# Query projections of a fused attention and feed-forward kernel in bursts of eight heads

## The chip, the cores and the metric

The kernel runs on one core of a Trainium2 chip. The engines of that core have instruction streams of their own: TensorE (PE in the profile, with its weight loads listed as PEld), VectorE (DVE), ScalarE (ACT), GpSimd (POOL) and SyncE (SP, which here only issues DMAs). The metric is the time of one execution on the device, in microseconds (us); lower is better. Before the change it is 561.32 us, the median of three runs from 560.52 to 561.76.

## What is computed

```python
def reference(A_x, A_k_cache, A_v_cache, A_wq, A_wo, B_x, B_w_gate, B_w_up, B_w_down):
    ...
        W = min(4096, max(256, Sk // 4))            # 512
        rep = Hq // Hkv                             # 16 // 8
        q = (x @ wq).reshape(B, Sq, Hq, Dh)         # 2048 rows, 16 heads of 256
        k = jnp.repeat(k_cache[:, :, Sk - W:, :], rep, axis=1)
        v = jnp.repeat(v_cache[:, :, Sk - W:, :], rep, axis=1)
        scores = jnp.einsum("bhqd,bhkd->bhqk", q, k) * (Dh ** -0.5)
        p = softmax(scores, axis=-1)
        o = jnp.einsum("bhqk,bhkd->bhqd", p, v)
        return o.reshape(B, Sq, Hq * Dh) @ wo
    ...
    xn = _layernorm(x, axis=-1)                     # x is 2048 x 448
    s = _A_ref(xn, A_k_cache, A_v_cache, A_wq, A_wo)
    g = _silu((gelu(xn @ w_gate) * (xn @ w_up)) @ w_down)
    return x + s * g
```

Every row of x attends to the last 512 cached keys; two query heads share one key head. The attention result is multiplied by a gate from a feed-forward net and added to x.

## The kernel before

The 2048 rows are worked in four chunks of 512 (QC), each as four tiles of 128 rows (TPC). The first part of the program (about 127 us) is the layer norm and the feed-forward net: `gate_up` (matmuls L370) and `down` (L382) leave the gate's input in `gy`. `silu` (L499 on ACT, L500 and L502 on POOL) turns it into the gate, one tile at a time, during the attention part.

The attention part is one loop over i = 0 to 63: chunk c = i // 16, head i % 16. For each i, four steps t = 0 to 3 are written out by hand, in this order for TensorE:

- `scores(i, t)`: two matmuls (L420) of 128 query rows against 512 keys, into PSUM bank 4 or 5. ACT takes the exponentials and their row sum (L424) into one of NPR row buffers `pr`, DVE takes the reciprocal (L426) and scales the row buffer in place (L427), and SP issues a DMA transpose (L236) from the row buffer into `pT`. Each row buffer has its own DMA semaphore.
- at even t, from the third head on, `values` for a head two and a half heads back: four matmuls (L440) of the transposed probabilities with V, into a bank from a table of eight places (0, 6, 0, 6, 0, 1, 6, 6). DVE empties it into `oT` (L446).
- at odd t, from i = 6, half of `outproj`: four of the eight matmuls (L460) that multiply a group of four finished heads by wo, for one tile of rows, in bank 7. When the second half is through (t = 3), DVE copies or adds the bank to `acc` (L479, L481). After a chunk's last group POOL multiplies by the gate (L485) and adds the rows of x (L487) from the buffer `xr` into `ofin`. After the fourth tile POOL issues the store of the chunk's result and the load of the next chunk's rows into `xr` (`load_xr`, issued through L233).
- at t = 0 of every fourth head, i = 3, 7, ..., 59, `q_burst`: the queries of the next four heads. A burst has four units. A unit is 14 matmuls of 64 contracted rows (L406); they come in pairs that run side by side in the two halves of the array and fill two PSUM banks, 0 and 1 or 2 and 3. ACT copies both banks with one instruction of 1024 columns (L410) into `qT`, which holds six heads. One burst also stands before the loop.

The outputs of the last group of all (chunk 3, heads 12 to 15) are written out after the loop, with smaller DVE instructions (L469, L471) that write `ofin`, and stores of their own. Before them the loop's remaining five `values` and two `outproj` follow (L549 to L553).

Nothing is scheduled by a planner: each engine runs its instructions in the order of the source. `Rec` (L23) records every operation with the tiles it reads and writes, and puts semaphore waits where an operation needs another engine's result or a buffer that another engine still uses; a DMA that overwrites a tile waits for DMAs and engines that read it. Buffers of the attention part lie in the SBUF space of buffers of the feed-forward part.

Of the kernel before, what the change touches and what calls it, by code (L numbers as in the profile page):

```python
# [5 lines left out]
ACT = mybir.ActivationFunctionType  # L6
ALU = mybir.AluOpType
BF16 = mybir.dt.bfloat16
# [3 lines left out]
P = 128  # L12
# [129 lines left out]
def bass_recurrent_scan__sliding_block_cached__geglu_ffn__prompt_kernel(nc, A_x, A_k, A_v, A_wq, A_wo, B_x, B_wg, B_wu, B_wd, out):  # L142
    _, S, D = A_x.shape
    Hkv, Sk, Dh = A_k.shape[1], A_k.shape[2], A_k.shape[3]
    HD = A_wq.shape[1]
    Hq = HD // Dh
# [12 lines left out]
    with es:  # L159
        off = [16512]  # L160

        def sb(name, shape, dt, at=None):
            n = 4 if dt == F32 else 2
            for x in shape[1:]:
                n *= x
            if at is None:
                at = off[0]
                off[0] += (n + 31) // 32 * 32
            return R.place(name, shape, dt, at), at + (n + 31) // 32 * 32
# [24 lines left out]
        hb, ffn_end = sb("hb", [P, NHB, QC], BF16)  # L194


        NPT = 4
        qT, at = sb("qT", [P, 6, NE, QC], BF16, gu_at)
        oT = [None, None]
        oT[0], at = sb("oT0", [P, 4 * NE, QC], BF16, at)  # L200
        xr, at = sb("xr", [P, TPC, D], BF16, at)
        assert at <= x_at
        pT, at = sb("pT", [P, NPT, NJ, QC], BF16, x_at)
        pr = []
        while at + 2 * W <= d_at:
            t_, at = sb("pr%d" % len(pr), [P, W], BF16, at)
            pr.append(t_)
        at = hb_at
        while at + 2 * W <= ffn_end:
            t_, at = sb("pr%d" % len(pr), [P, W], BF16, at)  # L210
            pr.append(t_)
        NPR = len(pr)
        oT[1], at = sb("oT1", [P, 4 * NE, QC], BF16, d_at)
        acc, at = sb("acc", [P, TPC, D], F32, at)
        tmp, at = sb("tmp", [P, 2, D], F32, at)
        ofin, at = sb("ofin", [P, TPC, D], BF16, at)
        assert at <= hb_at, (at, hb_at)
        psum = es.enter_context(nc.psum_tensor("ps", [P, 8 * 512], F32))

        def bank(b, n=512):  # L220
            return psum[:, b * 512:b * 512 + n]
# [10 lines left out]
        def dma(eng, dst, src, w=(), r=(), after=(), lane=None):  # L232
            return R.op(eng, lambda e: e.dma_start(dst, src), r=r, w=w, dma=True, after=after, lane=lane)  # L233
# [159 lines left out]
        NI = NQC * Hq  # L393
        NG = NI // 4

        def q_burst(G):

            c, h0 = divmod(4 * G, Hq)
            for n in range(4):
                hp, e_ = divmod(n, 2)  # L400
                s, i = 2 * (n % 2) if G else (4, 0, 2, 0)[n], (4 * G + 2 * hp) % 6

                def run(e, hp=hp, e_=e_, s=s):
                    for k in range(NK):
                        for b, lo in ((s, 0), (s + 1, HP)):
                            ins = e.matmul(bank(b), lhsT=wq[lo:lo + HP, k, h0 // 2 + hp, e_ * P:(e_ + 1) * P],  # L406
                                           rhs=xnT[lo:lo + HP, c, k, :], start=k == 0, stop=k == NK - 1)
                    return ins
                pe(run, r=xn(c) + [("wq", lo, k) for lo in range(2) for k in range(NK)], w=[("ps", s), ("ps", s + 1)])
                act(lambda e, e_=e_, s=s, i=i: e.activation(  # L410
                    qT[:, i:i + 2, e_, :], psum[:, s * 512:(s + 2) * 512].rearrange("p (a q) -> p a q", a=2), ACT.Copy),
                    r=[("ps", s), ("ps", s + 1)], w=[("qT", i, e_), ("qT", i + 1, e_)])

        def scores(i, t):
            g, n = (i % Hq) // 2, i * TPC + t
            b, s = 4 + n % 2, n % NPR

            def run(e):
                for k in range(NE):
                    ins = e.matmul(bank(b), lhsT=qT[:, i % 6, k, t * P:(t + 1) * P], rhs=kT[:, g, k, :],  # L420
                                   start=k == 0, stop=k == NE - 1)
                return ins
            pe(run, r=[("kT", g), ("qT", i % 6, 0), ("qT", i % 6, 1)], w=[("ps", b)])
            act(lambda e: e.activation(pr[s][:, :], bank(b), ACT.Exp, scale=scale, accum_out=den[:, s:s + 1]),  # L424
                r=[("ps", b)], w=[("pr%d" % s,), ("den", s)])
            dve(lambda e: e.reciprocal(rden[:, s:s + 1], den[:, s:s + 1]), r=[("den", s)], w=[("rden", s)])  # L426
            dve(lambda e: e.tensor_scalar(pr[s][:, :], pr[s][:, :], rden[:, s:s + 1], None, op0=ALU.mult),  # L427
                r=[("pr%d" % s,), ("rden", s)], w=[("pr%d" % s,)])
            dmaT(pT[:, i % NPT, :, t * P:(t + 1) * P], pr[s][:, :], r=[("pr%d" % s,)], w=[("pT", i % NPT, t)], lane="p%d" % s)

# [19 lines left out]
        def outproj(G, t, part, half=None):  # L450

            n8 = 4 * NE
            lo, hi = (0, D) if half is None else (half * D // 2, (half + 1) * D // 2)
            b = ((2, 2), (3, 5), (7, 4), (0, 6))[t][half or 0] if G == NG - 1 else (7, 7, 7, 4)[t] if G == NG - 2 else 7
            c, h0 = divmod(4 * G, Hq)
            end = c == NQC - 1

            def run(e):
                for idx in part:
                    ins = e.matmul(bank(b, D)[:, lo:hi], lhsT=oT[G % 2][:, idx, t * P:(t + 1) * P],  # L460
                                   rhs=wo[:, h0 * NE + idx, lo:hi],
                                   start=idx == 0, stop=idx == n8 - 1)
                return ins
            pe(run, r=[("oT%d" % (G % 2), idx) for idx in part] + [("wo", h0 // 4)], w=[("ps", b)])
            if part[-1] < n8 - 1:
                return
            n = c * TPC + t
            if end and h0 == Hq - 4:
                dve(lambda e: e.tensor_tensor(tmp[:, t % 2, lo:hi], bank(b, D)[:, lo:hi], gy[:, n, lo:hi], ALU.mult),  # L469
                    r=[("ps", b), ("gy", n)], w=[("tmp", t % 2)])  # L470
                dve(lambda e: e.tensor_tensor(ofin[:, t, lo:hi], tmp[:, t % 2, lo:hi], acc[:, t, lo:hi], ALU.add),  # L471
                    r=[("tmp", t % 2), ("acc", t)], w=[("ofin", t, lo)])
                if t == TPC - 1:
                    dma("sync" if half else "scalar", o_view[:, c, t, lo:hi], ofin[:, t, lo:hi], r=[("ofin", t, lo)])
                elif half != 0:
                    dma("sync", o_view[:, c, t, :], ofin[:, t, :], r=[("ofin", t, 0), ("ofin", t, lo)])
                return
            if h0 == 0:
                dve(lambda e: e.tensor_copy(acc[:, t, :], bank(b, D)), r=[("ps", b)], w=[("acc", t)])  # L479
            else:  # L480
                dve(lambda e: e.tensor_tensor(acc[:, t, :], bank(b, D), acc[:, t, :], ALU.add),  # L481
                    r=[("ps", b), ("acc", t)], w=[("acc", t)])
            if h0 == Hq - 4 or end and h0 == Hq - 8:
                dst, key = (acc, ("acc", t)) if end else (ofin, ("ofin", t))
                pool(lambda e: e.tensor_tensor(tmp[:, t % 2, :], acc[:, t, :], gy[:, n, :], ALU.mult),  # L485
                     r=[("acc", t), ("gy", n)], w=[("tmp", t % 2)])
                pool(lambda e: e.tensor_tensor(dst[:, t, :], tmp[:, t % 2, :], xr[:, t, :], ALU.add),  # L487
                     r=[("tmp", t % 2), ("xr",)], w=[key])
                if t == TPC - 1 and not end:
                    dma("gpsimd", o_view[:, c, :, :], ofin[:, :, :], r=[("ofin", t) for t in range(TPC)])  # L490
                    load_xr(c + 1)

        def load_xr(c):
            dma("gpsimd", xr[:, :, :], x_view[:, c, :, :], w=[("xr",)])

        def silu(n):

# [23 lines left out]
                    load_piece()  # L521
        assert not pieces
        act(lambda e: e.activation(small[:, 2:3], small[:, 0:1], ACT.Exp), r=[("eps",)], w=[("warm",)])
        q_burst(0)
        load_xr(0)

        fill = {}
# [5 lines left out]
        for i in range(NI):  # L533
            for t in range(TPC):
                scores(i, t)
                if 4 * i + t in fill:
                    down(NQC - 1, *fill[4 * i + t])
                if t % 2 == 0 and 4 * i + t >= 10:
                    values(*pv.pop(0))
                if 6 <= i and t % 2:  # L540
                    outproj(*outs[0], range(2 * t - 2, 2 * t + 2))
                    if t == TPC - 1:
                        outs.pop(0)
                if t == 0 and i % 4 == 3 and i + 1 < NI:
                    q_burst(i // 4 + 1)
            if 7 <= i and (i - 7) % 3 == 0 and (i - 7) // 3 < NT:
                silu((i - 7) // 3)

# [41 lines left out]
```

## Time and profile before

| | |
|---|---|
| median of three runs | 561.32 us (560.52 to 561.76) |
| the profiled execution | 561.18 us; span from first to last instruction 559.4 us |
| granted TensorE clock | 1.0 throughout |
| L406 query matmuls | x896, 99.5 us busy |
| L420 score matmuls | x481 recorded (512 issued), 145.4 us busy |
| L440 value matmuls | x510 recorded (512 issued), 130.8 us busy |
| L460 output matmuls | x536, 116.3 us busy |
| L424 exponentials on ACT | x256, 597 ns each |
| L410 query copies on ACT | x64, 1024 ns each |
| L427 scaling on DVE | x256, 416 ns each |
| L446 evictions on DVE | x124, 682 ns each |
| L485, L487 on POOL | x16 each, 1035 and 1033 ns |
| DMA transposes pT<-pr | x256, issued by SP, 1216 ns median per issue, 2.4 us to landing |

Busy times of lines on TensorE overlap, since a matmul's end is modelled and the next one starts before it. A few matmul records are missing from the trace, so spacing is read from start to start. In the profile's rows, "x" is the number of instructions merged in one row, and the text in brackets is the idle time of the engine before it with what ended it; "issue" there stands for nothing that the profile shows. A timeline row begins with the start and the length of the (merged) row in us. A row of the chain of waits has the same two numbers.

### The profile page before, as it was taken

The numbers are of one execution on the slowest core, as the hardware profiler recorded it, in microseconds if no ns is written. First come the engines' busy times: TensorE is split into PE (matmuls) and PEld (weight loads), VectorE is DVE, ScalarE is ACT, GpSimd is POOL, SyncE is SP. The second block draws the span as 40 slices with busy tenths as digits, with TensorE's granted clock in tenths as the row PEclk, the third lists the DMA queues.
The fourth block names the chain that finished last, engine by engine and source line by source line (L and its number), as shares of the span: only waits on it lengthen the run. The fifth ranks groups of instructions, "written<-read, shape, count | busy, mean of one in ns | idle before, by whom it ended". The sixth has DMA issues, their size and how long they took to land.

```text
span 559.4 us, 9865 instructions
## 1 busy us (share of the span) xinstructions
PE 549.0 (98%) x3499; PEld 257.2 (46%) x3532; DVE 322.9 (58%) x835; ACT 296.1 (53%) x673; POOL 90.1 (16%) x125
## 2 busy tenths in 40 slices
PE   7999999999999999999999999999999999999997
PEld 3544444444444444444444444444444444444445
DVE  5636446143464847474846657484747484755674
ACT  4324233247655565556565656656565656565641
POOL 0232323200000111013501101232100021400023
PEclk9999999999999999999999999999999999999999
DMA  8994746972453435353664344445535353645352
GB/s 193 276 191 86 138 102 136 247 137 65 94 85 68 97 64 99 69 91 64 143 98 94 73 86 71 81 84 137 101 67 99 63 95 71 147 79 101 70 92 52
DMA packets 169552, 58.83 MB, mean 105 GB/s; under 512 B 160160, under 2 KB 166432, under 8 KB 169504
## 3 DMA queue, kind: packets, MB, share of 16 engines
q1 hardware_dynamic: 166208, 45.50, 44.2%
q0 software_dynamic: 3152, 12.65, 8.9%
q8 instruction: 28, 0.46, 0.4%
q14 instruction: 20, 0.16, 0.1%
q10 hardware_dynamic: 144, 0.06, 0.0%
HBM read 17.92 MB, written 1.84 MB: 35 GB/s over the span
## 4 chain that ended last, share of the span: by engine, by line
PE 95%; DMA 1%; DVE 1%; issue 1%; SPq 1%; ACT 0%
PE ps L440 20%; PE ps L420 19%; PE ps L406 18%; PE ps L460 16%; PE ps L370 15%; PE ps L382 8%; DMA wgu<-in_B_w_up_dram 1%; SPq L233 1%; DVE tmp L469 0%; DVE ofin L471 0%; DVE pr L427 0%; DVE oT L446 0%; DVE rden L426 0%; ACT pr L424 0%
## 5 line engine op out<-in xcount | busy, mean ns | idle before, releaser
L424 ACT ACTIVATE pr<-ps 128x512 bf16<-128x512 f32 x256 | 152.8, 597 | 116.6 <-PE ps L420 112.5
L420 PE MATMUL ps<-kT,qT 128*128 128x512 bf16 x481 | 145.4, 379 | 3.3 <-issue 2.5
L440 PE MATMUL ps<-pT,V 128*128 128x512 bf16 x510 | 130.8, 379 | 0.6 <-DVE rden L426 0.4
L426 DVE RECIPROCAL rden<-den 128x1 f32<-128x1 f32 x256 | 41.5, 162 | 152.4 <-ACT pr L424 134.3
L460 PE MATMUL ps<-wo,oT 128*128 128x448 bf16 (+1 forms) x536 | 116.3, 344 | 0.0
L427 DVE TENSOR_SCALAR pr<-pr,rden 128x512 bf16<-128x512 bf16 x256 | 106.4, 416 | 9.0
L406 PE MATMUL ps<-xnT,wq 64*128 64x512 bf16 x896 | 99.5, 376 | 0.0
L410 ACT ACTIVATE qT<-ps 128x1024 bf16<-128x1024 f32 x64 | 65.5, 1024 | 49.8 <-PE ps L406 49.8
L370 PE MATMUL ps<-xnT,wgu 64*128 64x512 bf16 x784 | 85.5, 376 | 1.0 <-ACT xnT L322 0.8
L446 DVE CAST oT<-ps 128x512 bf16<-128x512 f32 x124 | 84.6, 682 | 0.6 <-PE ps L440 0.5
L440 PEld LDWEIGHTS ps<-pT,V 128*128 128x128 bf16 x512 | 49.9, 98 | 60.8 <-issue 1.2
L460 PEld LDWEIGHTS ps<-wo,oT 128*128 128x128 bf16 x536 | 52.3, 98 | 51.1
L420 PEld LDWEIGHTS ps<-kT,qT 128*128 128x128 bf16 x512 | 48.5, 98 | 57.1 <-issue 7.3
L376 DVE TENSOR_TENSOR actT<-ps,hb 128x512 bf16<-128x512 f32 x56 | 38.1, 685 | 57.5 <-ACT hb L374 55.7
L406 PEld LDWEIGHTS ps<-xnT,wq 64*128 64x128 bf16 x896 | 42.4, 94 | 55.9 <-DVE acc L481 4.2
L374 ACT ACTIVATE hb<-ps 128x512 bf16<-128x512 f32 x56 | 33.4, 597 | 51.8 <-PE ps L370 51.8
L370 PEld LDWEIGHTS ps<-xnT,wgu 64*128 64x128 bf16 x784 | 39.2, 94 | 46.5 <-issue 2.5
L424 ACT ACTIVATION_READ_ACCUMULATOR pr<-ps 128x1 f32 x256 | 49.9, 195 | 0.0
L500 POOL TENSOR_SCALAR tmp<-tmp 128x448 f32<-128x448 f32 x16 | 9.1, 572 | 233.9 <-ACT tmp L499 233.9
L382 PE MATMUL ps<-wd,actT 128*128 128x448 bf16 x224 | 46.2, 353 | 0.1
L485 POOL TENSOR_TENSOR tmp<-acc,gy 128x448 f32<-128x448 f32 x16 | 16.6, 1035 | 123.2 <-DVE acc L481 123.2
L382 PEld LDWEIGHTS ps<-wd,actT 128*128 128x128 bf16 x224 | 21.7, 98 | 22.2 <-issue 1.3
(43 smaller groups left out, 171.7 us busy)
## 6 DMA issues: line engine op xcount, KB each, us to landing
pT<-pr SPq DMA_TRANSPOSE x256, 2.4
wq<-in_A_wq_dram POOLq DMA_DIRECT2D x14, 256.0 KB, 4.3
wo<-in_A_wo_dram POOLq DMA_DIRECT2D x4, 896.0 KB, 10.1
V<-in_A_v_cache_dram POOLq DMA_DIRECT2D x4, 512.0 KB, 5.8
xr<-in_A_x_dram POOLq DMA_DIRECT2D x4, 448.0 KB, 4.8
wd<-in_B_w_down_dram SPq DMA_DIRECT2D x1, 1568.0 KB, 17.6
wgu<-in_B_w_gate_dram SPq DMA_DIRECT2D x3, 448.0 KB, 10.3
wgu<-in_B_w_up_dram SPq DMA_DIRECT2D x3, 448.0 KB, 11.8
```

Of the source, the lines that this page charges most:

```text
L370: ins = e.matmul(bank(b), lhsT=wgu[lo:lo + HP, k, f * P:(f + 1) * P], rhs=xnT[lo:lo + HP, c, k, :], start=k == 0, stop=k == NK - 1)
L376: dve(lambda e: e.tensor_tensor(actT[:, f, :], bank(s + 1), hb[:, n % NHB, :], ALU.mult), r=[("ps", s + 1), ("hb", n % NHB)], w=[("actT", f)])
L382: pe(lambda e, f=f: e.matmul(bank(b, D), lhsT=actT[:, f, t * P:(t + 1) * P], rhs=wd[:, f, :], start=f == 0, stop=f == NF - 1), r=[("actT", ...
L406: ins = e.matmul(bank(b), lhsT=wq[lo:lo + HP, k, h0 // 2 + hp, e_ * P:(e_ + 1) * P], rhs=xnT[lo:lo + HP, c, k, :], start=k == 0, stop=k == ...
L410: act(lambda e, e_=e_, s=s, i=i: e.activation(qT[:, i:i + 2, e_, :], psum[:, s * 512:(s + 2) * 512].rearrange("p (a q) -> p a q", a=2), AC ...
L420: ins = e.matmul(bank(b), lhsT=qT[:, i % 6, k, t * P:(t + 1) * P], rhs=kT[:, g, k, :], start=k == 0, stop=k == NE - 1)
L424: act(lambda e: e.activation(pr[s][:, :], bank(b), ACT.Exp, scale=scale, accum_out=den[:, s:s + 1]), r=[("ps", b)], w=[("pr%d" % s,), ("de ...
L426: dve(lambda e: e.reciprocal(rden[:, s:s + 1], den[:, s:s + 1]), r=[("den", s)], w=[("rden", s)])
L427: dve(lambda e: e.tensor_scalar(pr[s][:, :], pr[s][:, :], rden[:, s:s + 1], None, op0=ALU.mult), r=[("pr%d" % s,), ("rden", s)], w=[("pr%d ...
L440: ins = e.matmul(bank(b), lhsT=V[:, j, g, e_ * P:(e_ + 1) * P], rhs=pT[:, i % NPT, j, :], start=j == 0, stop=j == NJ - 1)
L446: dve(lambda e: e.tensor_copy(dst, bank(b)), r=[("ps", b)], w=[key])
L460: ins = e.matmul(bank(b, D)[:, lo:hi], lhsT=oT[G % 2][:, idx, t * P:(t + 1) * P], rhs=wo[:, h0 * NE + idx, lo:hi], start=idx == 0, stop=id ...
```

## The change

- `q_burst` takes the first head and a number of heads. The burst before the loop and the one at i = 3 still make four heads; from i = 7 on a burst stands only at i = 7, 15, ..., 55 and makes eight. There are nine bursts instead of sixteen; the units, their matmuls and their copies are the same in number, and banks 0 to 3 alternate as before.
- The queries have five buffers of a head pair each (`qT0` to `qT4`, ten heads) in place of one of six heads. Three lie where `qT` was, two at the end of the space of the feed-forward part.
- `ofin` is gone. POOL's sum (L487), and DVE's sums of the last group (L471), are written into `xr` in place, and the stores read `xr`. The load of the next chunk's rows overwrites the buffer that the store just before it on the same queue reads.
- The row buffers are laid out anew by `fill_pr`: there are ten (NPR) instead of nine.

```diff
--- before.py
+++ after.py
@@ -194,27 +194,32 @@
         hb, ffn_end = sb("hb", [P, NHB, QC], BF16)
 
 
-        NPT = 4
-        qT, at = sb("qT", [P, 6, NE, QC], BF16, gu_at)
+        NPT, NQP = 4, 5
+        qT = [None] * NQP
         oT = [None, None]
+        at = gu_at
+        for n in range(3):
+            qT[n], at = sb("qT%d" % n, [P, 2, NE, QC], BF16, at)
         oT[0], at = sb("oT0", [P, 4 * NE, QC], BF16, at)
         xr, at = sb("xr", [P, TPC, D], BF16, at)
-        assert at <= x_at
+        pr = []
+
+        def fill_pr(at, end):
+            while at + 2 * W <= end:
+                t_, at = sb("pr%d" % len(pr), [P, W], BF16, at)
+                pr.append(t_)
+
+        fill_pr(at, x_at)
         pT, at = sb("pT", [P, NPT, NJ, QC], BF16, x_at)
-        pr = []
-        while at + 2 * W <= d_at:
-            t_, at = sb("pr%d" % len(pr), [P, W], BF16, at)
-            pr.append(t_)
-        at = hb_at
-        while at + 2 * W <= ffn_end:
-            t_, at = sb("pr%d" % len(pr), [P, W], BF16, at)
-            pr.append(t_)
-        NPR = len(pr)
+        fill_pr(at, d_at)
         oT[1], at = sb("oT1", [P, 4 * NE, QC], BF16, d_at)
         acc, at = sb("acc", [P, TPC, D], F32, at)
         tmp, at = sb("tmp", [P, 2, D], F32, at)
-        ofin, at = sb("ofin", [P, TPC, D], BF16, at)
-        assert at <= hb_at, (at, hb_at)
+        for n in range(3, NQP):
+            qT[n], at = sb("qT%d" % n, [P, 2, NE, QC], BF16, at)
+        assert at >= hb_at, (at, hb_at)
+        fill_pr(at, nc.sbuf_usable_end)
+        NPR = len(pr)
         psum = es.enter_context(nc.psum_tensor("ps", [P, 8 * 512], F32))
 
         def bank(b, n=512):
@@ -393,12 +398,19 @@
         NI = NQC * Hq
         NG = NI // 4
 
-        def q_burst(G):
-
-            c, h0 = divmod(4 * G, Hq)
-            for n in range(4):
+        def q_slot(i):
+
+            p = i // 2
+            p = p if p < 3 else (p - 3) % NQP
+            return qT[p], "qT%d" % p, i % 2
+
+        def q_burst(i0, heads):
+
+            c, h0 = divmod(i0, Hq)
+            for n in range(heads):
                 hp, e_ = divmod(n, 2)
-                s, i = 2 * (n % 2) if G else (4, 0, 2, 0)[n], (4 * G + 2 * hp) % 6
+                s = 2 * (n % 2) if i0 else (4, 0, 2, 0)[n]
+                buf, name, _ = q_slot(i0 + 2 * hp)
 
                 def run(e, hp=hp, e_=e_, s=s):
                     for k in range(NK):
@@ -407,20 +419,21 @@
                                            rhs=xnT[lo:lo + HP, c, k, :], start=k == 0, stop=k == NK - 1)
                     return ins
                 pe(run, r=xn(c) + [("wq", lo, k) for lo in range(2) for k in range(NK)], w=[("ps", s), ("ps", s + 1)])
-                act(lambda e, e_=e_, s=s, i=i: e.activation(
-                    qT[:, i:i + 2, e_, :], psum[:, s * 512:(s + 2) * 512].rearrange("p (a q) -> p a q", a=2), ACT.Copy),
-                    r=[("ps", s), ("ps", s + 1)], w=[("qT", i, e_), ("qT", i + 1, e_)])
+                act(lambda e, e_=e_, s=s, buf=buf: e.activation(
+                    buf[:, :, e_, :], psum[:, s * 512:(s + 2) * 512].rearrange("p (a q) -> p a q", a=2), ACT.Copy),
+                    r=[("ps", s), ("ps", s + 1)], w=[(name, e_)])
 
         def scores(i, t):
             g, n = (i % Hq) // 2, i * TPC + t
             b, s = 4 + n % 2, n % NPR
+            buf, name, a = q_slot(i)
 
             def run(e):
                 for k in range(NE):
-                    ins = e.matmul(bank(b), lhsT=qT[:, i % 6, k, t * P:(t + 1) * P], rhs=kT[:, g, k, :],
+                    ins = e.matmul(bank(b), lhsT=buf[:, a, k, t * P:(t + 1) * P], rhs=kT[:, g, k, :],
                                    start=k == 0, stop=k == NE - 1)
                 return ins
-            pe(run, r=[("kT", g), ("qT", i % 6, 0), ("qT", i % 6, 1)], w=[("ps", b)])
+            pe(run, r=[("kT", g), (name, 0), (name, 1)], w=[("ps", b)])
             act(lambda e: e.activation(pr[s][:, :], bank(b), ACT.Exp, scale=scale, accum_out=den[:, s:s + 1]),
                 r=[("ps", b)], w=[("pr%d" % s,), ("den", s)])
             dve(lambda e: e.reciprocal(rden[:, s:s + 1], den[:, s:s + 1]), r=[("den", s)], w=[("rden", s)])
@@ -468,12 +481,12 @@
             if end and h0 == Hq - 4:
                 dve(lambda e: e.tensor_tensor(tmp[:, t % 2, lo:hi], bank(b, D)[:, lo:hi], gy[:, n, lo:hi], ALU.mult),
                     r=[("ps", b), ("gy", n)], w=[("tmp", t % 2)])
-                dve(lambda e: e.tensor_tensor(ofin[:, t, lo:hi], tmp[:, t % 2, lo:hi], acc[:, t, lo:hi], ALU.add),
-                    r=[("tmp", t % 2), ("acc", t)], w=[("ofin", t, lo)])
+                dve(lambda e: e.tensor_tensor(xr[:, t, lo:hi], tmp[:, t % 2, lo:hi], acc[:, t, lo:hi], ALU.add),
+                    r=[("tmp", t % 2), ("acc", t)], w=[("xr", t, lo), ("xr", t)])
                 if t == TPC - 1:
-                    dma("sync" if half else "scalar", o_view[:, c, t, lo:hi], ofin[:, t, lo:hi], r=[("ofin", t, lo)])
+                    dma("sync" if half else "scalar", o_view[:, c, t, lo:hi], xr[:, t, lo:hi], r=[("xr", t, lo)])
                 elif half != 0:
-                    dma("sync", o_view[:, c, t, :], ofin[:, t, :], r=[("ofin", t, 0), ("ofin", t, lo)])
+                    dma("sync", o_view[:, c, t, :], xr[:, t, :], r=[("xr", t, 0), ("xr", t, lo)])
                 return
             if h0 == 0:
                 dve(lambda e: e.tensor_copy(acc[:, t, :], bank(b, D)), r=[("ps", b)], w=[("acc", t)])
@@ -481,17 +494,17 @@
                 dve(lambda e: e.tensor_tensor(acc[:, t, :], bank(b, D), acc[:, t, :], ALU.add),
                     r=[("ps", b), ("acc", t)], w=[("acc", t)])
             if h0 == Hq - 4 or end and h0 == Hq - 8:
-                dst, key = (acc, ("acc", t)) if end else (ofin, ("ofin", t))
+                dst, key = (acc, ("acc", t)) if end else (xr, ("xr", t))
                 pool(lambda e: e.tensor_tensor(tmp[:, t % 2, :], acc[:, t, :], gy[:, n, :], ALU.mult),
                      r=[("acc", t), ("gy", n)], w=[("tmp", t % 2)])
                 pool(lambda e: e.tensor_tensor(dst[:, t, :], tmp[:, t % 2, :], xr[:, t, :], ALU.add),
-                     r=[("tmp", t % 2), ("xr",)], w=[key])
+                     r=[("tmp", t % 2), ("xr", t)], w=[key])
                 if t == TPC - 1 and not end:
-                    dma("gpsimd", o_view[:, c, :, :], ofin[:, :, :], r=[("ofin", t) for t in range(TPC)])
+                    dma("gpsimd", o_view[:, c, :, :], xr[:, :, :], r=[("xr", t) for t in range(TPC)])
                     load_xr(c + 1)
 
         def load_xr(c):
-            dma("gpsimd", xr[:, :, :], x_view[:, c, :, :], w=[("xr",)])
+            dma("gpsimd", xr[:, :, :], x_view[:, c, :, :], w=[("xr", t) for t in range(TPC)])
 
         def silu(n):
 
@@ -521,7 +534,7 @@
                     load_piece()
         assert not pieces
         act(lambda e: e.activation(small[:, 2:3], small[:, 0:1], ACT.Exp), r=[("eps",)], w=[("warm",)])
-        q_burst(0)
+        q_burst(0, 4)
         load_xr(0)
 
         fill = {}
@@ -541,8 +554,8 @@
                     outproj(*outs[0], range(2 * t - 2, 2 * t + 2))
                     if t == TPC - 1:
                         outs.pop(0)
-                if t == 0 and i % 4 == 3 and i + 1 < NI:
-                    q_burst(i // 4 + 1)
+                if t == 0 and (i == 3 or i % 8 == 7) and i + 1 < NI:
+                    q_burst(i + 1, 4 if i == 3 else 8)
             if 7 <= i and (i - 7) % 3 == 0 and (i - 7) // 3 < NT:
                 silu((i - 7) // 3)
```

## The prediction

> **What bounds the kernel now.** First the page's busy shares, the chain that ended last, and the queues.
>
> ```profile
> PE 549.0 (98%) x3499; PEld 257.2 (46%) x3532; DVE 322.9 (58%) x835; ACT 296.1 (53%) x673; POOL 90.1 (16%) x125
> ...
> q8 instruction: 28, 0.46, 0.4%
> ...
> PE 95%; DMA 1%; DVE 1%; issue 1%; SPq 1%; ACT 0%
> ...
> pT<-pr SPq DMA_TRANSPOSE x256, 2.4
> ```
>
> TensorE is on 95% of the chain. The attention part is a period of 26.12 us for four heads (the burst of L406 starts at 277.20, 303.32, 329.45). Removing work elsewhere pays only if TensorE waits for it; adding a wait costs only where TensorE then finds something missing. So I read next the timeline around one burst, for TensorE alone.
>
> ```profile
> 302.37 1.03 PE L440 MATMUL ps<-pT,V 128*128 128x512 bf16 x4
> 303.32 6.22 PE L406 MATMUL ps<-xnT,wq 64*128 64x512 bf16 x56
> 309.70 0.38 PE L420 MATMUL ps<-kT,qT 128*128 128x512 bf16 x1 [0.16 <-issue]
> ```
>
> Matmuls of 512 columns start 0.216 us apart (the trace's starts), two of 64 rows together. Four from 302.37 leave TensorE free at 303.23; the burst starts 0.09 later. Its 28 pairs take 6.05, to 309.37. The score pair shows one record where two matmuls were issued, so its first began 0.216 before 309.70, at 309.48: 0.11 late. **One burst costs 0.20 us of switching.** Cross-check: a period holds 92 slots of 0.216 and 32 of 0.189, 25.92 us; 26.12 less that is 0.20.
>
> Next, what the bursts cover. The table of PSUM banks in `values` gives bank 6 to two groups in succession, those at t=0 and t=2 of every head i with i%4=3. The burst stands between them, except at the last head, 63, where no burst follows. There the trace already shows the case that the change creates:
>
> ```profile
> 538.38 1.03 POOL L485 TENSOR_TENSOR tmp<-acc,gy 128x448 f32<-128x448 f32 x1 [53.63 <-DVE acc L481]
> ...
> 538.60 0.96 DVE L427 TENSOR_SCALAR pr<-pr,rden 128x512 bf16<-128x512 bf16 x1
> 539.48 0.68 DVE L446 CAST oT<-ps 128x512 bf16<-128x512 f32 x1
> ...
> 539.53 0.59 PE L420 MATMUL ps<-kT,qT 128*128 128x512 bf16 x2
> 540.52 0.81 PE L440 MATMUL ps<-pT,V 128*128 128x512 bf16 x3 [0.40 <-DVE rden L426]
> 541.16 0.59 PE L420 MATMUL ps<-kT,qT 128*128 128x512 bf16 x2
> ```
>
> The L420 pair ends its slots at 539.53+0.43=539.96, four L440 should take 0.86, so the next L420 was due at 540.82; it came at 541.16. **TensorE lost 0.34 us** because L446 emptied bank 6 late, and that because L427 took 0.96 instead of 0.35 while POOL ran L485. The same two lines at heads 51 and 59:
>
> ```profile
> 460.23 0.96 DVE L427 TENSOR_SCALAR pr<-pr,rden 128x512 bf16<-128x512 bf16 x1
> 461.11 0.68 DVE L446 CAST oT<-ps 128x512 bf16<-128x512 f32 x1
> ...
> 512.47 0.35 DVE L427 TENSOR_SCALAR pr<-pr,rden 128x512 bf16<-128x512 bf16 x1
> 512.74 0.68 DVE L446 CAST oT<-ps 128x512 bf16<-128x512 f32 x1
> ```
>
> At 51 the eviction ends 2.03 us after its last matmul started, as at 63; at 59, 1.42. The loss at 63 puts the limit at 2.03-0.34=1.69. Heads 11, 19 and 35 show 0.96 too (198.99, 251.24, 355.73); 27 and 43 show 0.35.
>
> Last, the queue of DMA transposes on SP, one for each of 256 rows of probabilities.
>
> ```profile
> 520.83 12.98 SPq L236 DMA_TRANSPOSE pT<-pr  x10
> ...
> 494.71 21.68 SPq L236 DMA_TRANSPOSE pT<-pr  x16
> ...
> 543.25 3.56 SPq L236 DMA_TRANSPOSE pT<-pr  x2
> ...
> 548.13 0.15 issue
> ```
>
> Ten issues in 12.98, the last 1.22 long, are 1.307 us apart (1.309 where no wait comes between). Outside a burst the scores come every 1.242 us (heads start 4.97 apart). So **SP falls behind by 0.067 per transpose, 1.07 per four heads, and catches up only in a burst.** The pair at 543.25 takes 3.56 instead of 2.53: one packet of q8, an instruction fetch, lies in that window, and the slow issues (2.05 to 2.33 long) sit at such fetches. Near the end the last transpose starts at 545.60 and lands 2.44 later, at 548.04; the L440 group that reads it begins within the stretch after 548.13. TensorE already waits for it, by 0.1 us: there any further delay counts in full.
>
> **The change part by part.** No matmul, copy, exponential or transpose is added or removed: the program has the same 3532 matmuls, 64 copies (L410) and 256 transposes. Moved: the second halves of seven bursts; the bursts at i=11, 19, 27, 35, 43, 51, 59 go, those at 7, 15, ..., 55 double.
>
> Switching: 7 x 0.20 = **-1.42** (0.203 unrounded). If the missing record were no matmul, the exit would cost 0.33 and the saving be 2.9; if the gaps came back elsewhere, 0. The period's cross-check speaks for 0.20.
> The Trainium skill (TensorE: Matmul & The Clock Gate, The mechanism) has weight loads overlap running matmuls only where their row groups differ. The trace differs: full-array loads of L460 run at 296.00 to 296.69 while full-array matmuls run, and the loads pause for 0.42 us at the switch. By that rule a switch is no dearer than any other load, the saving is nothing, and the sum below would be +3.3.
>
> Inside a doubled burst units 3 to 8 wait for the copy two units earlier instead of units 3 and 4 alone. A copy ends at 306.07 (305.05+1.02), its bank's next unit starts at 306.34 (303.32 + 14 x 0.216): 0.27 to spare, so nothing; were that cover gone, what the copy exceeds it by, six times a burst.
>
> Bank 6 without a burst: of the seven places four are late as at head 63 (11, 19, 35, 51), three 0.27 early. 4 x 0.34 = **+1.37**. Bounds: 0, if the order of POOL and DVE shifts by a third of a us, and 7 x 0.34 = 2.4.
> The Trainium skill (SBUF — State Buffer, SBUF: two separate sides) says that VectorE in a two-port mode and GpSimd exclude each other for a whole instruction. The row adds 0.61 to a scale; by the rule it could be all of L485, 1.03, so 0.76 lost per place, 3.0 in all, and the sum below +3.5.
>
> SP's queue at the end: in the present run the last transpose of the stretch before head 59's burst starts at 494.71+21.68-1.22=515.17, so SP is free for the next at 516.48. That next one starts at 520.83 as soon as its data is there; without the burst (6.05+0.20) it would be there at 514.58. SP is 1.90 late, 1.07 from the four more heads and 0.84 from one fetch (498.62). The page's 28 fetches for its 7,031 TensorE rows make one per about 250 instructions; counted on from the present ones, the changed order has them in the doubled burst at 55 (hidden) and at head 58 (not), so again one. After 520.83 SP has no idle time until the end, so nothing is recovered: **+1.90** on the landing that TensorE waits for. Bounds: 1.07 (no fetch) to 2.9 (two).
>
> Transposes in mid-run: the smallest margins from last landing to first L440 matmul with no burst between are 2.06 (head 16) and 2.3 (heads 20 and 32). The second half of a stretch carries 0.9 to 2.0 more lag, less 0.34 where TensorE stalled. I take nothing, upper bound 1.
>
> xr in place of ofin: load_xr on POOL now waits for the store (median 4.3 us to landing) that it was issued 0.6 behind. Queued behind it stand the two POOL steps of one silu (L500, L502); who waits is that chunk's gy, needed a dozen heads later, and the next rows, needed thirteen heads (some 80 us) later; POOL next sat idle 19.47 us. Nothing; without that idle time, up to 4.3 on three occasions. DVE's final sums (L471) write xr, long loaded: nothing. A tenth row buffer instead of nine only loosens a wait.
>
> Sum: -1.42 + 1.37 + 1.90 = +1.85. The profiled execution took 561.18 (span 559.4 and 1.8 around it), 0.14 under the median of 561.32: 563.0, and **563.2** on the median's footing.
>
> **The rivals.**
> *TensorE alone counts*: longer bursts give DVE and SP a deeper reserve, the waits land in slack, only the switches remain: 561.32-1.42=559.9. For it: 0.4 us of waiting on L440 in the whole run. Against: that 0.4 is exactly the uncovered place, and the reserve is used up 32 transposes later. It decides if the four evictions end within 1.69 and the last landing is no later.
> *The end hides it*: switches and evictions cancel (-0.05), the last transposes are only 0 to 1 late: 561.3 to 562.3. For: one fetch more or less is 0.84 to 1.1. Against: SP's unbroken chain from 520.83.
> *SP breaks through in mid-run*: heads 20, 36, 52 wait as well, 0.3 to 1 us together with a second fetch: 563.8 to 565. Against: stalls there give SP time back.
>
> **How the numbers follow.** Forecast 0.53 (562.5 to 563.7), SP in mid-run 0.13, end hidden 0.22, TensorE alone 0.12. 0.2% is 1.1 us, what a measurement of this kernel can tell from no change: faster below 560.2, slower above 562.4. Faster 0.12, same 0.22, slower 0.66. The range takes in the forecast, the hidden end and most of the upper rival: 560.8 to 564.6; the slower cases alone, 562.4 to 564.6.
>
> **What would show it.** L406 in nine runs, seven of 112; L440 waits of a third of a us at four places besides head 63, on L446 or the DVE line after it; SP's issues without idle time from after head 55's burst; the last landing some 2 us later against the outproj before it. Wrong if L440 shows no new waits, or SP idles between heads 55 and 63.

## The result, and the profile after

The changed kernel takes 562.85 us (median of nine runs, 562.02 to 563.40) against 561.30 before (nine runs, 560.52 to 561.76). The ratio is 1.0029, with a 95% interval from 1.0020 to 1.0038: slower, by 1.55 us. The profiled execution took 563.40 us, the longest of the nine; its span is 561.6.

Lines have moved: the query matmuls are L418 (were L406), the scores L433 (L420), the values L453 (L440), the output matmuls L473 (L460), the scaling L440 (L427), the eviction L459 (L446), the transposes L241 (L236).

The page of the kernel after: busy shares, the chain's shares by engine, and the group of the value matmuls, whose last part is TensorE's idle time before them and what ended most of it.

```profile
PE 549.8 (98%) x3499; PEld 258.2 (46%) x3532; DVE 322.5 (57%) x835; ACT 296.9 (53%) x673; POOL 90.1 (16%) x125
...
PE 91%; DMA 3%; DVE 3%; SPq 2%; issue 1%; ACT 0%
...
L453 PE MATMUL ps<-pT,V 128*128 128x512 bf16 x497 | 129.3, 379 | 4.3 <-DMA pT<-pr 2.0
```

The number of instructions is the same. TensorE's share of the chain fell from 95% to 91%, and what took its place is the DMA, VectorE and SP. The waits of TensorE say where (us in total, times, longest):

```profile
PE ps L453 <- DMA pT<-pr: 2.0, 2, 1.4
PE ps L453 <- DVE rden L439: 1.8, 5, 0.4
```

Before, the second kind stood there once (0.4 us, at head 63) and the first not at all. Five waits on a VectorE line are head 63 and four new places. One of them, head 51, in the timeline of TensorE:

```profile
467.50 0.59 PE L433 MATMUL ps<-kT,qT 128*128 128x512 bf16 x2
468.49 0.81 PE L453 MATMUL ps<-pT,V 128*128 128x512 bf16 x3 [0.39 <-DVE rden L439]
469.13 0.59 PE L433 MATMUL ps<-kT,qT 128*128 128x512 bf16 x2
```

And of VectorE:

```profile
466.57 0.96 DVE L440 TENSOR_SCALAR pr<-pr,rden 128x512 bf16<-128x512 bf16 x1
467.45 0.68 DVE L459 CAST oT<-ps 128x512 bf16<-128x512 f32 x1
```

The scaling takes 0.96, the eviction of bank 6 ends at 468.13, and the score matmuls that should start at 467.50+6x0.216=468.80 start at 469.13: 0.33 late. At head 27, where the scaling is quick, the same place shows nothing (scores at 311.06, values at 311.71, scores at 312.36, where the first record of the four is missing).

A burst of eight heads is dense from end to end:

```profile
276.85 1.03 PE L453 MATMUL ps<-pT,V 128*128 128x512 bf16 x4
277.80 12.26 PE L418 MATMUL ps<-xnT,wq 64*128 64x512 bf16 x112
290.22 0.38 PE L433 MATMUL ps<-kT,qT 128*128 128x512 bf16 x1 [0.16 <-issue]
```

It has the entry and the exit of a burst of four (0.09 and 0.11 us) around 56 pairs instead of 28.

The end, in the chain of waits (start, length, what):

```profile
544.09 1.22 SPq L241
...
545.39 2.32 SPq L241
...
547.80 2.44 DMA pT<-pr
550.25 0.25 issue
550.50 1.89 PE ps L453 x8
```

Before, this stretch of the chain was TensorE's L460 until 548.13. Now it is the row of DMA transposes: TensorE finished its L473 before at 548.91 (the last of eight started at 548.72, 0.189 each) and stood until the last transpose landed at 550.24.

How the time divides is seen best from three marks in each trace, the first burst (before the loop), the burst at head 55, and the end of the span. The start differs by up to 1 us between these executions (the first burst starts at 126.33 to 127.35, in e9, with more work ahead of it, at 128.15), so stretches are compared. Medians of different groups of runs compare only to about half a us: the kernel before, which ran in each, had medians of 561.30, 561.47, 561.01 and 561.12. Here are all the runs.

| kernel | median us | first burst to burst 55 | burst 55 to end |
|---|---|---|---|
| before | 561.30 | 359.50 | 73.21 |
| after | 562.85 | 359.57 | 75.00 |
| bank table (e1) | 561.34 | 358.22 | 74.78 |
| last burst split (e2) | 561.31 | 359.57 | 72.88 |
| both (e3) | 559.64 | 358.22 | 72.93 |
| bursts of four, rest as after (e4) | 560.72 | 359.50 | 72.90 |
| e4 with one burst of eight at the end (e5) | 563.26 | 359.50 | 74.95 |
| after, one wait less per transpose (e6) | 563.01 | 359.58 | 74.68 |
| e1, one wait less (e7) | 561.22 | 358.22 | 73.80 |
| e3, one wait less (e8) | 559.44 | 358.22 | 72.72 |
| after, fetches shifted (e9) | 563.26 (one run) | 359.58 | 73.73 |
| e4 with nine row buffers (e10) | 561.39 | 359.50 | 73.66 |

In the change itself six of the seven switches are saved before head 55 and all four late evictions lie there: together +0.07. The rest, +1.79, is the end.

### The profile page after: what moved, and what is told of

It is laid out like the page before. It is cut to its first block, busy times and chain, and to the rows that moved or that the text cites. A ratio compares the mean times of both kernels' runs of the same rounds, so it can differ in the third digit from the quotient of the medians.

```text
span 561.6 us, 9863 instructions
## 1 busy us (share of the span) xinstructions
PE 549.8 (98%) x3499; PEld 258.2 (46%) x3532; DVE 322.5 (57%) x835; ACT 296.9 (53%) x673; POOL 90.1 (16%) x125
## 4 chain that ended last, share of the span: by engine, by line
PE 91%; DMA 3%; DVE 3%; SPq 2%; issue 1%; ACT 0%
PE ps L433 19%; PE ps L453 18%; PE ps L418 17%; PE ps L473 15%; PE ps L375 14%; PE ps L387 8%; DMA wgu<-in_B_w_up_dram 2%; SPq L238 1%; DVE pr L440 1%; SPq L241 1%; DVE oT L459 1%; DVE tmp L482 0%; DMA pT<-pr 0%; DVE xr L484 0%; DVE rden L439 0%
## 5 line engine op out<-in xcount | busy, mean ns | idle before, releaser
L433 PE MATMUL ps<-kT,qT 128*128 128x512 bf16 x494 | 148.2, 379 | 1.9 <-issue 1.4
L453 PE MATMUL ps<-pT,V 128*128 128x512 bf16 x497 | 129.3, 379 | 4.3 <-DMA pT<-pr 2.0
L473 PE MATMUL ps<-wo,oT 128*128 128x448 bf16 (+1 forms) x536 | 116.3, 344 | 0.0
L440 DVE TENSOR_SCALAR pr<-pr,rden 128x512 bf16<-128x512 bf16 x256 | 106.0, 414 | 9.0
L418 PE MATMUL ps<-xnT,wq 64*128 64x512 bf16 x896 | 98.3, 376 | 0.0
L459 DVE CAST oT<-ps 128x512 bf16<-128x512 f32 x124 | 84.6, 682 | 0.6 <-PE ps L453 0.5
L453 PEld LDWEIGHTS ps<-pT,V 128*128 128x128 bf16 x512 | 49.6, 98 | 64.5 <-issue 6.1
L473 PEld LDWEIGHTS ps<-wo,oT 128*128 128x128 bf16 x536 | 52.4, 98 | 51.1
L433 PEld LDWEIGHTS ps<-kT,qT 128*128 128x128 bf16 x512 | 49.1, 98 | 55.7 <-issue 4.5
L418 PEld LDWEIGHTS ps<-xnT,wq 64*128 64x128 bf16 x896 | 43.0, 94 | 54.6 <-DVE acc L492 1.7
```

The source lines that it names most:

```text
L433: ins = e.matmul(bank(b), lhsT=buf[:, a, k, t * P:(t + 1) * P], rhs=kT[:, g, k, :], start=k == 0, stop=k == NE - 1)
L453: ins = e.matmul(bank(b), lhsT=V[:, j, g, e_ * P:(e_ + 1) * P], rhs=pT[:, i % NPT, j, :], start=j == 0, stop=j == NJ - 1)
L459: dve(lambda e: e.tensor_copy(dst, bank(b)), r=[("ps", b)], w=[key])
```

## The experiments

Intervals are 95%, of the ratio to the kernel before, which ran beside each group (medians 561.47 for e1 to e4, 561.01 for e5 to e8, 561.12 for e9 and e10). Diffs are against the changed kernel unless another is named.

**The bank table (e1).** Where no burst stands between, banks 0 and 6 alternate.

```diff
-            b = (0, 6, 0, 6, 0, 1, 6, 6)[at % 8] if at < 2 * NI else (0, 6, 0, 6, 1)[at - 2 * NI]
+            row = (0, 6, 0, 6, 0, 1, 6, 6) if at < 8 or at % 16 > 7 and at < 120 else (0, 6, 0, 6, 0, 6, 0, 6)
+            b = row[at % 8] if at < 2 * NI else (0, 6, 0, 6, 1)[at - 2 * NI]
```

> The changed kernel (562.85), with bank 6 no longer used twice running where no burst stands between (heads i%8=3 from 11 on, and 63). Theory (three terms: seven switches saved, -1.5; four late evictions, +1.37; SP's queue at the end, +1.9): the four L453 waits of a third of a us go, 561.5; the wait at head 63 goes too but is handed on to the last transposes, for nothing. Rival A (SP's queue alone makes the loss, and it has slack only through those stalls): 562.6 to 562.9. Rival B (the store that the next load waits for, and the new buffer places, make the loss): 562.85.

561.34 us (ratio 0.9997, 0.9976 to 1.0017). The waits on VectorE are gone. At head 19, where the changed kernel lost 0.34, TensorE now runs through:

```profile
257.99 0.59 PE L433 MATMUL ps<-kT,qT 128*128 128x512 bf16 x2
258.43 1.03 PE L454 MATMUL ps<-pT,V 128*128 128x512 bf16 x4
259.29 0.59 PE L433 MATMUL ps<-kT,qT 128*128 128x512 bf16 x2
```

Among the waits of TensorE this line has stayed:

```profile
PE ps L454 <- DMA pT<-pr: 2.1, 2, 1.5
```

The stretch to head 55 is 1.35 shorter than after, 0.34 for each of four places, and 1.28 shorter than before, 0.21 for each of six switches saved. Rival A, for which these waits were free, falls. The end is 0.22 shorter, where nothing was expected: the last transpose is issued 60.99 after the start of burst 55 instead of 61.19 (the two slow issues among the last 34 take 4.26 together instead of 4.38). The rest of the 0.34 that head 63 no longer loses is waited out at the last transposes, whose waits grew from 2.0 to 2.1.

**The last burst split (e2).**

```diff
-                if t == 0 and (i == 3 or i % 8 == 7) and i + 1 < NI:
-                    q_burst(i + 1, 4 if i == 3 else 8)
+                if t == 0 and (i == 3 or i % 8 == 7 or i == 59) and i + 1 < NI:
+                    q_burst(i + 1, 4 if i in (3, 55, 59) else 8)
```

> The changed kernel with the last eight heads' queries in two bursts of four, at heads 55 and 59, as before. Theory: the last transposes come 1.9 us sooner and one switch of 0.2 is paid: 561.15. Rival A: the same 561.1, but then with the evictions' waits worth nothing in e1. Rival B: 563.0 (a switch more, nothing gained).

561.31 us (0.9993, 0.9983 to 1.0004). The stretch to head 55 is as after to a hundredth, the end 2.12 shorter. Of the waits of the value matmuls only the five of the bank table are left, none on a transpose:

```profile
PE ps L453 <- DVE rden L439: 0.9, 5, 0.2
```

In this row the recorded idle time of such a place is 0.18 where the row after has 0.39: the first matmul behind the wait is in the record here and missing there. The loss is the same, since the stretch is.

**Both (e3).** The two edits together (the bank table keeps 6, 6 at head 59, where a burst stands again).

> Both edits: the bank table without immediate reuse, and the last eight heads in two bursts of four. Theory: six switches saved and no new wait: 562.85 - 1.37 - 1.7 = 559.8, that is 1.3 to 1.5 under the kernel before. Rival A: 561.1. Rival B: 562.9.

559.64 us (0.9967, 0.9954 to 0.9980): faster than before and after. The two causes add up: 562.85 less 1.51 (e1) less 1.54 (e2) is 559.80.

**All but the schedule (e4).**

```diff
-                if t == 0 and (i == 3 or i % 8 == 7) and i + 1 < NI:
-                    q_burst(i + 1, 4 if i == 3 else 8)
+                if t == 0 and i % 4 == 3 and i + 1 < NI:
+                    q_burst(i + 1, 4)
```

> Everything of the change but the bursts' places: five pair buffers, ten row buffers, the sums in the rows' buffer with the load behind the store, and bursts of four at every fourth head. Theory: these cost nothing: 561.3, within 0.3. Rival B: they are the loss: 562.8 or more.

560.72 us (0.9986, 0.9976 to 0.9996). Rival B falls: the buffers, the sums in the rows' buffer and the load that waits for the store cost nothing. They even save some 0.6 us; what the two traces show of it, 0.31, lies behind head 55 (72.90 against 73.21). e10 looks into that.

**Of the schedule, only its last step (e5).** Against e4:

```diff
-                if t == 0 and i % 4 == 3 and i + 1 < NI:
-                    q_burst(i + 1, 4)
+                if t == 0 and i % 4 == 3 and i < 59:
+                    q_burst(i + 1, 8 if i == 55 else 4)
```

> Bursts of four as before up to head 51, and then one of eight at head 55, none at 59: of the change only its last step, which has no late eviction (head 59 is one of the three in time). Theory: one switch saved and the last transposes 1.9 us later than with a burst at 59: 560.7 (all but the schedule) - 0.2 + 1.9 = 562.4. A rival in which the end's wait comes of the whole run's lag, not of the last stretch: 560.5.

563.26 us (1.0035, 1.0022 to 1.0049): this one step brings the whole loss. It misses the expected 562.4 by 0.9. In the traces the end is 2.05 longer than e4's where 1.7 was expected; 0.3 of that is the length of one slow transpose, 2.23 us here and 1.93 in e4. The rest of the difference between the medians is not in these two traces.

**One wait less per transpose (e6, e7, e8).** A transpose waits for the one before it from the same row buffer and for the one before into the same place of pT. Both follow from its other waits.

```diff
-            if lane in self.lanes:
+            if lane in self.lanes and lane[0] != "p":
...
-            if k in self.writer:
+            if k in self.writer and not (k[0] == "pT" and self.readers.get(k)):
```

> The changed kernel with one wait less before each DMA transpose of the probabilities: that for the transpose before on the same row buffer and on the same place of pT, which the other waits imply. In the trace an issue is 1.217 us and 0.092 more pass to the next, 0.046+0.017 of them around a wait of its own. Theory (SP's rate of issue sets the end): an interval of about 1.25 instead of 1.309, some 1.5 to 2 us less lag over the last 34 issues, so 561.0 to 561.4, the four late evictions unchanged. If the rate is set by the transfers and not by SP's instructions: interval 1.309 and 562.85.

563.01 us (1.0029, 1.0009 to 1.0049): no gain, the second case. The two kernels' transposes, after first (last three numbers: shortest, median and longest issue in ns):

```profile
L241 SPq DMA_TRANSPOSE pT<-pr x256: 1188/1216/2592, 135.5 to 547.8; - x128
```

And with one wait less:

```profile
L241 SPq DMA_TRANSPOSE pT<-pr x256: 1188/1264/2572, 135.6 to 547.5; - x128
```

The 0.048 us by which the pause between two issues got shorter is added to the issue itself. Ten undisturbed issues in a row in the kernel after, and eleven in the one with one wait less:

```profile
520.52 12.99 SPq L241 DMA_TRANSPOSE pT<-pr  x10
...
519.48 14.35 SPq L241 DMA_TRANSPOSE pT<-pr  x11
```

Less the last issue, that is nine intervals of 1.308 and ten of 1.309: the interval stays. So the wait does not set it. That the transfers do, as the second case has it, is not shown either: in both traces the packets of one transpose (queue q1) mostly end 0.39 us before those of the next begin. What holds the issue is open.

On the bank table:

> The bank table without immediate reuse and one wait less per transpose, bursts of eight to the end. Theory: nothing but the seven saved switches and a last landing no later than before: 559.3 to 559.7. If the interval stays: 561.3, as with the bank table alone.

561.22 us (0.9999, 0.9985 to 1.0013), the second case again. Its shorter end in the table (73.80, e1 has 74.78) is no gain of the wait. The profiled execution, 560.15, is 1.07 under the run's median, and in it the last instruction fetch of TensorE (more on these at e9) stands at 548.2, behind the last issue at 544.48; in e1, with the same TensorE instructions, it stands at 543.2, beside an issue of 2.36.

On both edits:

> The same with the last eight heads' queries in two bursts of four. Theory: 559.3 to 559.6, the same as with one burst of eight, since a switch more costs 0.2 and the shorter last stretch has at most that to give. If the interval stays: 559.6, as without.

559.44 us (0.9965, 0.9952 to 0.9978), the same as e3 within the spread.

**Moving the instruction fetches (e9).**

```diff
+                for _ in range(100):
+                    ins = e.matmul(bank(3, 64), lhsT=actT[:, NF - 1, 0:P], rhs=actT[:, NF - 1, 0:64], start=True, stop=True)
```

> The changed kernel with 100 more small matmuls (64 columns, zeros, result unused) at the start, 200 TensorE instructions that move every later instruction fetch 200 instructions earlier against the work. In the changed kernel two fetches fall between the last burst (head 55) and the end, at heads 58 and 63; shifted, the first falls into that burst and the second at about head 59, so one is left. The time itself is not comparable (the start is some us longer); read from the first L418 burst to the end. Theory (a fetch costs the transposes about 1 us and nothing makes it good): the last transpose is 3.5 instead of 4.5 us behind its scaling, and burst to end is 433.6 instead of 434.6 us. If the slow issues have another cause: 4.5 and 434.6.

From the first mark to burst 55 nothing changes (359.58); the end is 73.73, 1.27 shorter than after, so burst to end is 433.3 where 433.6 was expected. The timeline of SP in the last stretch of the kernel after, and three issues around head 58; one packet of q8, an instruction fetch, stands between 515.5 and 517.5:

```profile
502.46 46.56 SPq L241 DMA_TRANSPOSE pT<-pr  x34
...
514.42 4.70 SPq L241 DMA_TRANSPOSE pT<-pr  x3
```

The same 34 issues with the fetches shifted, and the three around the one fetch before the last issue (one packet of q8 between 525 and 527.5):

```profile
503.58 45.30 SPq L241 DMA_TRANSPOSE pT<-pr  x34
...
524.53 4.70 SPq L241 DMA_TRANSPOSE pT<-pr  x3
```

Three issues take 2x1.309+1.22=3.83 where nothing disturbs them; with a fetch among them 4.70 in both kernels. One fetch less in the stretch, and its 34 issues take 1.26 less: the slow issues come with the fetches, and each is paid in full at the end. The last transpose was issued 3.26 behind its scaling, against 4.53 after.

**Nine row buffers instead of ten (e10).** e4 with `NPR = 9`.

> Bursts of four with the change's buffers, as in the run that was 0.14% under the kernel before, but with nine row buffers used instead of ten. If the tenth buffer made those 0.7 us: 561.3. If they lie in the spread between runs, or in the rows' buffer: 560.7.

561.39 us (1.0002, 0.9992 to 1.0012): as the kernel before, so by the medians the 0.7 us go with the tenth buffer; the intervals of e4 and e10 just touch. The last three issues of this run and of e4, one fetch among them in each:

```profile
541.87 5.30 SPq L241 DMA_TRANSPOSE pT<-pr  x3
```

In e4:

```profile
541.59 4.55 SPq L241 DMA_TRANSPOSE pT<-pr  x3
```

The slow issue at the fetch is 0.75 longer in e10 (2.68 against 1.93), as much as the two ends differ (73.66 and 72.90). That the buffer makes this difference is not shown: the slow issue at this fetch takes 2.25 in the kernel before, which has nine buffers too, and 1.59 (e2) to 2.36 (e1) in kernels with ten. How a tenth buffer saves time is open.

## Why the prediction was right, step by step

*Sum and direction.* +1.85 was forecast, 563.2; measured +1.55, 562.85. Between the two profiled executions the part behind the first burst grew by 1.86; that this meets the sum to a hundredth is luck, since the profiled execution after was the longest of its nine and two sizes that were off made up for each other (below).

*Switching*, -1.42. e1 shows 1.28 for six, 0.213 each, 1.49 for seven (e4, with the same buffers and all sixteen bursts, has the 359.50 of the kernel before). The missing record was a matmul, as the cross-check with the period had it: an exit of 0.33 would have given 0.42. The trace of e4 has the record (last row below): 28 pairs from 303.10 take 6.05, and the scores start 0.10 later. The Trainium skill (TensorE: Matmul & The Clock Gate, The mechanism) lets weight loads overlap running matmuls only where their row groups differ. What the prediction worked out from that, a switch no dearer than any other weight load, falls with the 0.213 of e1.

```profile
303.10 6.22 PE L418 MATMUL ps<-xnT,wq 64*128 64x512 bf16 x56
309.25 0.61 PE L433 MATMUL ps<-kT,qT 128*128 128x512 bf16 x2
```

*Evictions*, +1.37. Four places, those named, 0.34 each; e1 takes 1.35 back. The three quick places lost nothing. The Trainium skill (SBUF — State Buffer, SBUF: two separate sides) has VectorE in a two-port mode and GpSimd exclude each other for a whole instruction. The scalings of 0.96 us beside POOL instructions of 1.03, and of 0.35 without, fit that, but the upper estimate worked out from it was 3.0; the row at head 63 was the better one.

*The end*, +1.90. The last transpose is issued 4.53 behind its scaling (before: 2.53), and the waits follow: +1.79 after the saved switch, so 2.0. e2 takes both parts away together, and e5 brings both. Apart they were sized less well than the sum: one fetch was put at 0.84 and costs 1.27 (e9); the four heads, put at 1.07, come to 1.04 (the end of e9 over that of e4, with one fetch beside a late issue in each, is 0.83, and a switch of 0.21 is saved). That makes 2.3 over e4, whose end is 0.31 shorter than that of the kernel before, and so the 2.0. These are single traces. A second fetch fell near head 58, where the count of instructions had put it.

*What was taken as nothing.* Inside the doubled burst no unit waits. In mid-run no transpose is late: the smallest margin left is 1.5 us (heads 41 and 52). POOL does wait for the stores, three times, 9.3 us in all, and nobody waits for POOL. All this is as forecast, except the tenth row buffer: "only loosens a wait" missed some 0.6 us, by e4 and, less surely, e10, in the end's favour. That is why the three terms over the buffers alone come to 2.13 (562.85 less 560.72) and the sum over the kernel before to 1.55.

*Where a reason behind a right number was weak.* The prediction took the interval of 1.309 us from the rows and gave no reason for it. That the wait between two issues makes up part of it was the expectation of e6, and is refuted; the interval stood.

The rivals: "TensorE alone counts" is the state that e3 comes near, with both new waits removed; the change as it stands is far from it. "The end hides it" falls with e2 and e5. "SP breaks through in mid-run" did not happen.

## What to carry to other kernels

A burst of work on the engine that sets the pace is also a pause for everything behind it. Before merging two bursts, list what each pause covers (a PSUM bank used twice running, a queue that is slower than the loop and catches up only there) and look for the place where the pause is already absent: here head 63 gave the price of one cover to a hundredth of a us. A queue whose rate is below the loop's builds lag in every stretch. Here it cost nothing until the last one, since 1.5 us of margin stayed in mid-run; so the last pause is kept near the end and the others are merged. With the bank table mended as well, that is e3, at 559.64.

## What the runs showed that was not expected

Taking one wait away from each transpose shortened the pause between two issues from 0.093 to 0.044 us and lengthened the issue from 1.216 to 1.264: the interval of 1.309 us is not set by that wait, nor do the packets fill it. The instruction fetches of TensorE (16 KB, one per some 250 of its instructions) make the DMA transpose beside them longer, mostly by about 1 us (2.06 and 2.32 instead of 1.22 in the last stretch after, 2.68 in e10), so the place of a fetch in the instruction stream moves the end of this kernel by a us. With the same instructions it need not come at the same time in every execution (the last one at 543.2 in e1 and 548.2 in e7).
